# Pooled attention followed by a mixture-of-depths layer, one core: operations on different banks of one PSUM tile are declared independent

## The chip, the cores and the metric

The kernel runs on one core of one Trainium2 chip. The metric is the time of one launch on the device in microseconds (us). A second figure, the span, runs from the first to the last profiled instruction of the same execution.

## What is computed

The reference takes q, k and v of shape 8 batches x 8 heads x 576 tokens x 64. Keys and values are averaged over groups of 8 tokens, so each query attends to 72 pooled rows. The result, with the heads put side by side, is a row of 512 numbers per token; in each batch the 128 tokens with the highest gate score go through a small MLP, and its output is added to them.

```python
k_p = k.reshape(B, H, Sp, pool, D).mean(axis=3)
v_p = v.reshape(B, H, Sp, pool, D).mean(axis=3)
scores = scale * np.matmul(q, k_p.transpose(0, 1, 3, 2))
attn = np.exp(scores - max); attn = attn / (attn.sum + 1e-09)
x = (attn @ v_p).transpose(0, 2, 1, 3).reshape(B, S, 512)
scores = np.einsum('bsd,d->bs', x, w_gate)
for b in range(B):
    top_idx = np.argpartition(-scores[b], capacity)[:capacity]
    xe = x[b, top_idx]
    ye = np.maximum(xe @ w1, 0.0) @ w2
    g = 1.0 / (1.0 + np.exp(-scores[b, top_idx]))
    out[b, top_idx] = x[b, top_idx] + g[:, None] * ye
```

(w1 is 512 x 1024 and w2 is 1024 x 512; all data are float32.)

## The kernel before, in words

Everything that runs in this case is in `direct_path`; `general_path` stands behind a branch that the data do not take. Each batch b passes two parts. The front (`front(b)`) pools k (L507 on TensorE for batch 0, L518 and L519 on VectorE or GpSimd otherwise), transposes k and q (L527, L549), makes the scores in two halves (L567, L576), exponentiates them on ScalarE (L581, L585), pools v (L599, or L609 to L619), multiplies (L644, L648), divides by the row sums (`zs` L662 to L666, the reciprocal L670, `norm` L679 on ScalarE or L681 on VectorE), stores the 512-wide rows, and ranks the tokens: `score` (L697, L698), `spread` on TensorE (L718), a copy of the spread scores into `sr` (L398 on ScalarE, L400 on VectorE), five counts (L730), a one-hot matrix (L737, L741), `pick` on TensorE (L747), then `token` (L751), `value` (L764), the row numbers (L755) and a gather of the chosen rows by GpSimd (L756). The dense part (`dense(b)`) transposes the gathered rows (`turn`, L777), copies them (`xg`, L398 or L400), multiplies with w1 (`up`, L786), applies the maximum with 0 (`relu`, L793 on ScalarE, L795 on VectorE), multiplies with w2 (`down`, L800), forms `y` on VectorE (L805) and scatters it by GpSimd (`put`, L809). A put waits for the put before it. At the very end eight small matmuls (`busy`, L828), a check of ranges (L835 to L848) and a branch follow.

The order of all operations, the PSUM bank of each job and the engine of those that may run on two are a written table (ORDER, HOMES, TURNS); `Plan.place` walks it and issues operation after operation, and each engine executes its own in that order. A job is a chain of operations on the same bank or banks: TensorE writes, then VectorE or ScalarE reads.

PSUM has eight banks, held in three tiles: `pG` is banks 0 to 3, `pA` banks 4 and 5, `pJ` banks 6 and 7. `single(j)` and `pair(j)` give the view of a job's bank. Which instruction must wait for which is not written in the kernel: the recording layer derives it from the tiles that each instruction reads and writes. In the kernel before, an instruction on one bank of `pG` waits for an earlier instruction of another engine on another bank of `pG` just as for one on its own bank; the same holds for `pA` and `pJ`.

Of the kernel before, what the change touches and what calls it, by code (L numbers as in the profile page):

```python
# [101 lines left out]
ON_PE = (0,)  # L102


class Plan:
# [125 lines left out]
    def place(self):  # L231
# [10 lines left out]
        for n in order:  # L242
            e = ops[n]["eng"]
            self.before = last.get(e)
            if ops[n]["alts"]:
                ops[n]["fn"](e)
            else:
                ops[n]["fn"]()
            last[e] = ops[n]["mark"]


def direct_path(ctx, tc, q, k, v, moe_w_gate, moe_w1, moe_w2, moe_capacity, out, flag):
# [117 lines left out]

    out_rows = out.rearrange("b s d -> (b s) d")
# [127 lines left out]
    def pool_k(b):  # L499
        x = KR.rearrange("p (r t) d -> p r t d", t=4)  # L500
        if b in ON_PE:
            for n, (a, z) in enumerate(((0, 5), (5, 9))):
                j_ = plan.job(ONES)

                def sums(a=a, z=z, j_=j_):
                    for t in range(4):
                        nc.tensor.matmul(single(j_)[:, 0 : D * (z - a)], ident, x[:, a:z, t], start=(t == 0), stop=(t == 3))  # L507
# [45 lines left out]
    def scores(b, h):  # L553
# [8 lines left out]
        def go():  # L562
            for j in range(2):
                for r in range(4):
                    rows = slice(32 * r, 32 * r + 32)
                    for s in range(2):
                        nc.tensor.matmul(pG[64 * s : 64 * s + 64, r, 0:n], KT[i][rows, j, s, 0:NK],  # L567
                                         tokens(j, s, rows, 0, hi - lo), start=(j == 0), stop=(j == 1))
        add("PE", 0.03 + n * 3.55e-3, go, [("KT", i), ("QT", i, h)], [], 100 * b + 10 * h, mode=3264, job=j_, name=f"s{b}{h}")

        def rest():
            for j in range(2):
                for s in range(2):
                    for u, (a, z) in enumerate(SUB[h]):
                        x = 64 * s + 32 * u
                        nc.tensor.matmul(pG[x : x + 32, 0, n : n + w], KL[i][:, j, s].rearrange("p n m -> p (n m)"),  # L576
                                         tokens(j, s, slice(0, 128), a - lo, z - lo), start=(j == 0), stop=(j == 1))
        add("PE", 0.05 + w * 3.35e-3, rest, [("KL", i), ("QT", i, h)], [], 100 * b + 10 * h, mode=12832, job=j_, name=f"sl{b}{h}")

        def ex():  # L580
            nc.scalar.activation(EM[h][i], pG[:, :, 0:n], AF.Exp, scale=exp_scale)  # L581
        add("ACT", 0.03 + 4 * n * 0.985e-3, ex, [], [("EM", h, i)], 100 * b + 5, job=j_, name=f"x{b}{h}")

        def exl():
            nc.scalar.activation(EL[h][i], pG[:, 0, n : n + w], AF.Exp, scale=exp_scale)  # L585
# [47 lines left out]
    def attend(b, c):  # L633
# [5 lines left out]
        def go():  # L639
            acc = pair(j_)  # L640
            for m in range(NP):
                for s in range(2):
                    for z in range(halves):
                        nc.tensor.matmul(acc[64 * z : 64 * z + 64, s, E * m : E * m + E], EM[h][i][64 * s : 64 * s + 64, m, m0 + 64 * z : m0 + 64 * z + 64],  # L644
                                         VS[i][64 * s : 64 * s + 64, m, :], start=(m == 0), stop=False, skip_group_check=True)
            for s in range(2):
                for z in range(halves):
                    nc.tensor.matmul(acc[64 * z : 64 * z + 64, s, 0 : NP * E], EL[h][i][64 * s : 64 * s + 64, l0 + 64 * z : l0 + 64 * z + 64],  # L648
                                     VL[i][64 * s : 64 * s + 64, u].rearrange("p m e -> p (m e)"),
                                     start=False, stop=True, skip_group_check=True)  # L650
# [7 lines left out]
        def zs(e):  # L658
            o = view()
            z, g = (x.rearrange("p (s m) -> p s m", s=2) for x in (ZA[rows, b, c], SS[i][rows, c]))  # L660
            if e == "ACT":
                nc.scalar.activation(z, o[:, :, :, D], AF.Identity, bias=eps[rows])  # L662
                nc.scalar.copy(out=g, in_=o[:, :, :, D + 1])
            else:
                nc.vector.tensor_scalar(z, o[:, :, :, D], 1e-9 * POOLW, None, op0=OP.add)
                nc.vector.tensor_copy(g, o[:, :, :, D + 1])  # L666
# [6 lines left out]
        def norm(e):  # L673
            rz, o = RZ[i][rows, c], view()
            to = XS[i][c][rows].rearrange("p (m s d) -> p s m d", s=2, d=D)
            if e == "ACT":
                for s in range(2):
                    for m in range(NP):
                        nc.scalar.activation(to[:, s, m], o[:, s, m, 0:D], AF.Copy, scale=rz[:, NP * s + m : NP * s + m + 1])  # L679
            else:  # L680
                nc.vector.tensor_tensor(out=to, in0=o[:, :, :, 0:D],  # L681
                                        in1=rz.rearrange("p (s m one) -> p s m one", s=2, one=1).to_broadcast([n, 2, NP, D]),
                                        op=OP.mult)
# [8 lines left out]
    def rank(b):  # L692
# [18 lines left out]
        for half, (a, z) in enumerate(((0, 3), (3, NC))):  # L711
# [33 lines left out]
        def pick():  # L745
            for c in range(NC):
                nc.tensor.matmul(single(j_)[0:cap, 0:5], OH[:, c, :], AUX[i][:, c, :], start=(c == 0), stop=(c == NC - 1))  # L747
        add("PE", 0.25, pick, ["OH", ("AUX", i)], [], p - 70, job=j_, name=f"pk{b}")

        def token():  # L750
            nc.vector.tensor_reduce(out=TK[x], in_=single(j_)[0:cap, 0:2], axis=AX.X, op=OP.add)  # L751
# [485 lines left out]
```

## Time and profile before

| | us |
|---|---|
| median of the 2 runs shown | 292.2 |
| lowest and highest of them | 290.26, 294.14 |
| the profiled execution, its own time | 293.1 |
| its span | 291.3 |
| TensorE busy in the span | 235.7 |
| VectorE busy in the span | 151.6 |

The profiled execution is 0.9 us over the median. Its time is the span and 1.8 us outside it. In the rows further down, PE is TensorE, PEld its loading of weights, DVE VectorE, ACT ScalarE, POOL GpSimd and SP the engine that only issues transfers. A row of the timeline gives a start, a length and in brackets the idle time of the engine just ahead of the instruction, with the instruction whose end released it. PEclk is the TensorE clock that was granted, 1.00 being 2.4 GHz and 0.50 being 1.2 GHz.

### The profile page before, as it was taken

What the parts mean: (1) busy time and instruction counts of PE and PEld (TensorE: products, weight loads), DVE (VectorE), ACT (ScalarE), POOL (GpSimd) and SP (SyncE); (2) the same over time, 40 slices, a digit from 0 to 9 for tenths busy, and PEclk for the clock granted to TensorE, in tenths of its full rate; (3) what the DMA queues carried; (4) which work ended last, traced back from release to release, by engine and by line L of the source; (5) the groups of instructions that cost most, each with busy time, mean ns of one, the idle gap of its engine ahead of it and who ended that gap; (6) DMA issues with size and microseconds to landing.
All of it is one profiled execution on the core that took longest, in us unless ns stands there. A gap on an engine that the chain in (4) does not pass through costs nothing.

```text
span 291.3 us, 7374 instructions
## 1 busy us (share of the span) xinstructions
PE 235.7 (81%) x3074; PEld 163.1 (56%) x3074; DVE 151.6 (52%) x346; ACT 89.2 (31%) x302; POOL 96.2 (33%) x154
## 2 busy tenths in 40 slices
PE   4789559975499798999969889989939998897680
PEld 4576328644278347847745458546828767384240
DVE  5039997938386485787681767484540180001310
ACT  1013461873226545402464333643120001101000
POOL 4004587418730551160634541330531100201310
PEclk9599956989599999999999999999986999999697
DMA  5996798999994556599576200140245000100201
GB/s 185 294 318 195 255 334 301 347 285 284 369 345 166 207 177 214 158 316 309 174 238 230 66 2 2 47 121 16 97 119 170 7 32 0 36 2 0 102 6 47
DMA packets 18413, 47.88 MB, mean 164 GB/s; under 512 B 2964, under 2 KB 2964, under 8 KB 17476
## 3 DMA queue, kind: packets, MB, share of 16 engines
q1 hardware_dynamic: 13776, 37.75, 40.1%
q0 software_dynamic: 2896, 6.76, 7.1%
q10 hardware_dynamic: 1700, 2.82, 3.2%
q8 instruction: 26, 0.43, 0.6%
q14 instruction: 15, 0.12, 0.1%
HBM read 35.78 MB, written 11.53 MB: 162 GB/s over the span
## 4 chain that ended last, share of the span: by engine, by line
PE 43%; issue 17%; DMA 10%; DVE 9%; POOL 4%; ACT 2%; ACTq 0%; SPq 0%; POOLq 0%; DVEq 0%
PE pJ L786 9%; PE pJ L800 8%; DMA xr<-out_dram,ix 6%; PE pG L786 4%; PE pG L800 4%; PE pG L567 4%; DMA out_dram<-y,ix 3%; PE pG L644 2%; PE pA L644 2%; PE pG L576 2%; PE pG L648 2%; DMA vr<-in_v_dram 1%; PE pA L648 1%; DVE y L805 1%; DVE ss L697 1%
## 5 line engine op out<-in xcount | busy, mean ns | idle before, releaser
L786 PE MATMUL pJ<-xg,w 128*128 128x128 f32 x352 | 44.2, 279 | 5.2 <-DVE ht L795 2.1
L786 PEld LDWEIGHTS pJ<-xg,w 128*128 128x128 f32 x352 | 41.2, 192 | 11.6 <-issue 4.0
L730 DVE SCALAR_TENSOR_TENSOR cmp<-sr,sc,lat 128x576 bf16<-128x576 f32 (+1 forms) x40 | 37.6, 940 | 4.9 <-ACT sr L398 4.2
L800 PE MATMUL pJ<-w,ht 128*128 128x512 f32 x64 | 29.9, 602 | 3.5 <-issue 2.1
L567 PE MATMUL pG<-qt,kt 32*64 32x256 f32 (+1 forms) x512 | 22.5, 451 | 3.6 <-issue 2.0
L549 DVE STREAM_TRANSPOSE qt<-qr 128x1280 f32<-128x1280 f32 (+1 forms) x16 | 21.7, 1361 | 2.1 <-DMA qr<-in_q_dram 2.1
L755 POOL TENSOR_SCALAR ix<-tk 128x1 int32<-128x1 f32 x8 | 2.3, 285 | 60.5 <-DVE tk L751 25.8
L800 PE MATMUL pG<-w,ht 128*128 128x512 f32 x32 | 17.5, 699 | 5.7 <-DVE y L805 4.8
L581 ACT ACTIVATE em<-pG 128x1280 f32<-128x1280 f32 (+1 forms) x16 | 18.1, 1129 | 8.4 <-PE pG L576 8.4
L800 PEld LDWEIGHTS pJ<-w,ht 128*128 128x128 f32 x64 | 11.3, 190 | 14.7 <-issue 12.6
L609 POOL TENSOR_TENSOR vr<-vr 128x512 f32<-128x512 f32 (+1 forms) x11 | 16.6, 1525 | 1.3 <-DMA vr<-in_v_dram 1.3
L809 POOL DMA_INDIRECT out_dram<-y,ix x8 | 8.4, 1048 | 26.2 <-DVE y L805 23.0
L567 PEld LDWEIGHTS pG<-qt,kt 32*64 32x64 f32 x512 | 10.5, 141 | 11.6 <-issue 7.4
L800 PE MATMUL pA<-w,ht 128*128 128x512 f32 x32 | 16.7, 625 | 0.0
L644 PEld LDWEIGHTS pG<-vs,em 64*64 64x64 f32 x528 | 12.5, 144 | 7.1 <-issue 2.3
L786 PE MATMUL pG<-xg,w 128*128 128x128 f32 x128 | 15.5, 277 | 1.0 <-ACT ht L793 0.7
L786 PEld LDWEIGHTS pG<-xg,w 128*128 128x128 f32 x128 | 14.9, 192 | 2.2 <-issue 1.0
L644 PE MATMUL pG<-vs,em 64*64 64x66 f32 x528 | 14.0, 234 | 2.2 <-DVE ss L666 0.7
L800 PEld LDWEIGHTS pG<-w,ht 128*128 128x128 f32 x32 | 6.9, 226 | 14.7 <-issue 8.0
L679 ACT ACTIVATE xs<-pA,rz 128x64 f32<-128x64 f32 (+1 forms) x64 | 14.0, 342 | 2.2 <-DVE rz L670 1.3
L679 ACT ACTIVATE xs<-pG,rz 128x64 f32<-128x64 f32 x48 | 10.5, 329 | 12.9 <-DVE xs L681 6.8
L644 PEld LDWEIGHTS pA<-vs,em 64*64 64x64 f32 x480 | 11.2, 139 | 3.8 <-issue 2.6
(173 smaller groups left out, 397.6 us busy)
## 6 DMA issues: line engine op xcount, KB each, us to landing
vr<-in_v_dram SPq DMA_DIRECT2D x32, 256.0 KB
kr<-in_k_dram SPq DMA_DIRECT2D x7, 1152.0 KB
qr<-in_q_dram SPq DMA_DIRECT2D x8, 640.0 KB
qr<-in_q_dram SPq DMA_DIRECT2D x8, 512.0 KB
w<-in_moe_w_dram SPq DMA_DIRECT2D x4, 1024.0 KB
out_dram<-xs SPq DMA_DIRECT2D x15, 256.0 KB
out_dram<-xs ACTq DMA_DIRECT2D x9, 256.0 KB
vr<-in_v_dram SPq DMA_DIRECT2D x32, 64.0 KB
```

What stands on the lines that cost most here:

```text
L549: nc.vector.transpose(out=QT[b % 2][h].rearrange("p j t c -> p t j c"), in_=QR[b % 2][h].rearrange("p t (j e) -> p t j e", j=2))
L567: nc.tensor.matmul(pG[64 * s : 64 * s + 64, r, 0:n], KT[i][rows, j, s, 0:NK], tokens(j, s, rows, 0, hi - lo), start=(j == 0), stop=(j == 1))
L576: nc.tensor.matmul(pG[x : x + 32, 0, n : n + w], KL[i][:, j, s].rearrange("p n m -> p (n m)"), tokens(j, s, slice(0, 128), a - lo, z - lo) ...
L581: nc.scalar.activation(EM[h][i], pG[:, :, 0:n], AF.Exp, scale=exp_scale)
L609: engine(e).tensor_tensor(out=x[:, a:z, 0:4], in0=x[:, a:z, 0:4], in1=x[:, a:z, 4:8], op=OP.add)
L644: nc.tensor.matmul(acc[64 * z : 64 * z + 64, s, E * m : E * m + E], EM[h][i][64 * s : 64 * s + 64, m, m0 + 64 * z : m0 + 64 * z + 64], VS[ ...
L648: nc.tensor.matmul(acc[64 * z : 64 * z + 64, s, 0 : NP * E], EL[h][i][64 * s : 64 * s + 64, l0 + 64 * z : l0 + 64 * z + 64], VL[i][64 * s ...
L679: nc.scalar.activation(to[:, s, m], o[:, s, m, 0:D], AF.Copy, scale=rz[:, NP * s + m : NP * s + m + 1])
L730: nc.vector.scalar_tensor_tensor(cmp[0:n], SR[0:n], SC[i][0:n, c : c + 1], LAT[0:n, LAST - OFF[c] : LAST - OFF[c] + S], op0=OP.subtract, o ...
L786: nc.tensor.matmul(single(ju)[:, cap * f : cap * f + cap], w1[g][:, d, 128 * f : 128 * f + 128], XG[i][:, d, :], start=(d == 0), stop=(d = ...
L800: nc.tensor.matmul(single(jd)[0:cap, :], HT[i][f // 4][:, f % 4, :], w2[f // 4][:, f % 4, :], start=(f == 0), stop=(f == FB - 1))
L809: j = nc.gpsimd.indirect_dma_start(out=out_rows, out_offset=bass.IndirectOffsetOnAxis(ap=IX[x][:, :1], axis=0), in_=Y[i], in_offset=None)
```

## The change

`Plan.place` now keeps, beside the operation that is being issued, its engine, its job and the operations that it needs by the plan. A new function `note` is called with each instruction that touches PSUM. It looks back over the last 500 noted instructions of the same PSUM tile, and where the earlier one ran on another engine, is not among the operations needed, and has no bank in common, it declares that there is no dependency between the two. The 30 or so places where PSUM is written or read are wrapped in `note(...)`; nothing else changes.

```diff
+AGO = 500
...
-            self.before = last.get(e)
+            self.before, self.now = last.get(e), (n, e, ops[n]["job"], ops[n]["deps"])
...
+    beside = {}
+
+    def note(ins):
+        n, e, j, needs = plan.now
+        if j is None:
+            return
+        mine = plan.bank[j]
+        seen_ = beside.setdefault(max(mine[0], 2) // 2, [])
+        for m, x, theirs, d in seen_[-AGO:]:
+            if e != d and m not in needs and not set(mine) & set(theirs):
+                tc.declare_no_dep(ins.ins, x.ins, reason="another bank")
+        seen_.append((n, ins, mine, e))
...
     def copy(e, to, of):
         if e == "ACT":
-            nc.scalar.copy(out=to, in_=of)
+            note(nc.scalar.copy(out=to, in_=of))
         else:
-            nc.vector.tensor_copy(to, of)
+            note(nc.vector.tensor_copy(to, of))
...
-                nc.tensor.matmul(single(jd)[0:cap, :], HT[i][f // 4][:, f % 4, :], w2[f // 4][:, f % 4, :],
-                                 start=(f == 0), stop=(f == FB - 1))
+                note(nc.tensor.matmul(single(jd)[0:cap, :], HT[i][f // 4][:, f % 4, :], w2[f // 4][:, f % 4, :],
+                                 start=(f == 0), stop=(f == FB - 1)))
...
-            nc.vector.scalar_tensor_tensor(Y[i], single(jd)[0:cap, :], GV[x], XR[x], op0=OP.mult, op1=OP.add)
+            note(nc.vector.scalar_tensor_tensor(Y[i], single(jd)[0:cap, :], GV[x], XR[x], op0=OP.mult, op1=OP.add))
```

No instruction is added, removed or moved on any engine; only the waits differ. In the built program 57 of TensorE's 1,635 instructions, 32 of VectorE's 305, 29 of ScalarE's 317, 2 of GpSimd's 153 and 3 of SP's 114 wait for something else than before. Part of these differences are waits that an earlier instruction of the engine took care of before, and that now stand at the instruction that truly needs them. The lines below the inserted code are 14 higher in the changed kernel (L800 becomes L814).

Three places show it. The rows name the engine whose progress is waited for, not the instruction. The first is TensorE from the last `up` of batch 7 to its `down`, the kernel's last large piece of work; `down` writes bank 3 of `pG`, and `y` of batch 6 reads bank 0 of it (`ht_144` and `ht_145` are the two halves of the relu's output). Before:

```order
L786 MATMUL pJ<-xg_141,w_148 128x128 x8
L800 MATMUL pA<-w_151,ht_145 128x512 x3
L800 MATMUL pG<-w_150,ht_144 128x512 [waits DVE_49]
L800 MATMUL pG<-w_150,ht_144 128x512 x3
L800 MATMUL pG<-w_151,ht_145 128x512 x4
```

and now:

```order
L800 MATMUL pJ<-xg_141,w_148 128x128 x8
L814 MATMUL pA<-w_151,ht_145 128x512 x3
L814 MATMUL pG<-w_150,ht_144 128x512 [waits Activation_49]
L814 MATMUL pG<-w_150,ht_144 128x512 x3
L814 MATMUL pG<-w_151,ht_145 128x512 [waits Activation_49]
L814 MATMUL pG<-w_151,ht_145 128x512 x3
```

Nothing moved. The wait for VectorE (for `y` of batch 6) is gone, and in its place stand the waits for the two relus of batch 7 on ScalarE.

The second is VectorE at the end: `value` and `token` of batch 7, then `y` of batches 4, 5, 6 and 7 with the reciprocals of their gates between them. Before:

```order
L764 TENSOR_REDUCE gv_135<-pG 128x1 [waits PE_49,Activation_49]
L751 TENSOR_REDUCE tk_127<-pG 128x1 [waits Activation_49]
L768 RECIPROCAL gv_132<-gv_132 128x1 [waits Pool_49]
L805 SCALAR_TENSOR_TENSOR y_146<-pA,gv_132,xr_136 128x512 [waits DMASW0_49,DMASW5_49,DVE_49,PE_49]
...
L805 SCALAR_TENSOR_TENSOR y_147<-pA,gv_133,xr_137 128x512 [waits DMASW2_49,DMASW1_49,DVE_49]
L805 SCALAR_TENSOR_TENSOR y_146<-pG,gv_134,xr_138 128x512 [waits DMASW6_49,DMASW0_49,Activation_49]
```

and now:

```order
L778 TENSOR_REDUCE gv_135<-pG 128x1 [waits PE_49]
L765 TENSOR_REDUCE tk_127<-pG 128x1
L782 RECIPROCAL gv_132<-gv_132 128x1 [waits Pool_49]
L819 SCALAR_TENSOR_TENSOR y_146<-pA,gv_132,xr_136 128x512 [waits DMASW5_49,DMASW0_49,DVE_49]
...
L819 SCALAR_TENSOR_TENSOR y_147<-pA,gv_133,xr_137 128x512 [waits DMASW1_49,DMASW2_49,DVE_49,PE_49]
L819 SCALAR_TENSOR_TENSOR y_146<-pG,gv_134,xr_138 128x512 [waits DMASW6_49,DMASW0_49]
```

Again the order is the same. `y` of batch 4, on bank 4, no longer waits for TensorE's last writes to bank 5, which are the `down` of batch 5; that wait now stands at `y` of batch 5, which reads them. `token` of batch 7 no longer waits for a relu on ScalarE.

The third is TensorE where batch 5 is turned and batch 7 is spread over `pG`, between the `up` of batch 4 and that of batch 5. Before:

```order
L786 MATMUL pG<-xg_140,w_149 128x128 x15
L777 MATMUL pG<-ident,xr_137 128x128 [waits DMASW1_49,Activation_49]
L777 MATMUL pG<-ident,xr_137 128x128 x3
L800 MATMUL pA<-w_150,ht_142 128x512 [waits DVE_49]
L718 MATMUL pG<-ident,sc_114 128x128 [waits DVE_49]
L718 MATMUL pG<-ident,sc_114 128x128 x2
L786 MATMUL pA<-xg_141,w_148 128x128 x8
```

and now:

```order
L800 MATMUL pG<-xg_140,w_149 128x128 x15
L791 MATMUL pG<-ident,xr_137 128x128 [waits DMASW1_49,Activation_49]
L791 MATMUL pG<-ident,xr_137 128x128 x3
L814 MATMUL pA<-w_150,ht_142 128x512 [waits DVE_49]
L732 MATMUL pG<-ident,sc_114 128x128 [waits DVE_49]
L732 MATMUL pG<-ident,sc_114 128x128 x2
L800 MATMUL pA<-xg_141,w_148 128x128 [waits DVE_49,Activation_49]
```

The spread's wait has kept its engine but not its instruction: before, it is for a relu (L795), the ninth VectorE instruction after the score sum of batch 7; now it is for that sum itself (L698, now L712). The turn's wait for ScalarE is unchanged, but the ScalarE instruction in front of it, `norm` of batch 7 (L679), no longer waits for the last matmul of the `up` of batch 4 on another bank of `pG`.

## Rows read from the trace of the kernel before

**Rows 1.** The page: span, busy time by engine, TensorE's clock and DMA by slices.

```profile
span 291.3 us, 7374 instructions
...
PE 235.7 (81%) x3074; PEld 163.1 (56%) x3074; DVE 151.6 (52%) x346; ACT 89.2 (31%) x302; POOL 96.2 (33%) x154
...
PEclk9599956989599999999999999999986999999697
DMA  5996798999994556599576200140245000100201
```

**Rows 2.** Windows: stretch, length, busy time by engine, PEclk, DMA share, GB/s.

```profile
20.00:44.00 24.00, 16.94 (x352) 10.91 (x352) 23.14 (x38) 10.81 (x41) 13.73 (x13) 0.83 0.83 270
44.00:78.00 34.00, 24.85 (x512) 18.29 (x511) 21.74 (x40) 16.18 (x65) 20.63 (x33) 0.80 0.99 313
95.00:200.00 105.00, 93.78 (x1434) 60.60 (x1434) 67.73 (x161) 44.17 (x153) 39.65 (x54) 1.00 0.48 157
200.00:267.31 67.31, 59.21 (x410) 44.26 (x401) 18.05 (x60) 8.40 (x23) 10.76 (x23) 0.95 0.17 52
217.55:223.42 5.87, 5.87 (x22) 4.84 (x23) 0.00 (x0) 0.68 (x2) 1.30 (x2) 0.50 0.58 178
267.31:272.11 4.80, 0.00 (x1) 0.01 (x1) 2.59 (x7) 0.60 (x1) 2.30 (x3) 0.91 0.14 55
272.11:278.03 5.92, 5.92 (x7) 2.52 (x8) 0.70 (x3) 0.00 (x0) 1.04 (x2) 0.50 0.23 89
278.03:282.17 4.14, 4.14 (x12) 1.88 (x11) 0.00 (x0) 0.00 (x0) 0.00 (x0) 1.00 0.00 0
```

**Rows 3.** Timeline of PE: seven instructions that stood behind a wait.

```profile
76.52 0.87 PE L777 MATMUL pA<-ident,xr 128*128 128x128 f32 x3 [6.60 <-DMA xr<-out_dram,ix]
97.69 0.67 PE L800 MATMUL pJ<-w,ht 128*128 128x512 f32 x1 [2.10 <-issue]
149.61 0.60 PE L786 MATMUL pJ<-xg,w 128*128 128x128 f32 x3 [2.07 <-DVE ht L795]
162.12 0.66 PE L777 MATMUL pJ<-ident,xr 128*128 128x128 f32 x4 [0.63 <-DMA xr<-out_dram,ix]
212.61 0.66 PE L777 MATMUL pG<-ident,xr 128*128 128x128 f32 x4 [1.83 <-ACT xs L679]
217.55 0.69 PE L718 MATMUL pG<-ident,sc 128*128 128x128 f32 x2 [3.42 <-DVE ht L795]
272.11 10.06 PE L800 MATMUL pG<-w,ht 128*128 128x512 f32 x16 [4.80 <-DVE y L805]
```

**Rows 4.** Timeline of DVE: four waits, then two of the counts.

```profile
19.11 0.42 DVE L400 COPY ks<-pG 128x256 f32<-128x256 f32 x1 [12.40 <-PE pG L599]
66.04 0.16 DVE L751 TENSOR_REDUCE tk<-pJ 128x1 f32<-128x2 f32 x1 [4.93 <-ACT sr L398]
267.34 0.75 DVE L805 SCALAR_TENSOR_TENSOR y<-pA,gv,xr 128x512 f32<-128x512 f32 x1 [18.95 <-PE pA L800]
282.21 0.75 DVE L805 SCALAR_TENSOR_TENSOR y<-pG,gv,xr 128x512 f32<-128x512 f32 x1 [9.36 <-PE pG L800]
...
113.43 0.81 DVE L730 SCALAR_TENSOR_TENSOR cmp<-sr,sc,lat 128x576 bf16<-128x576 f32 x1
145.25 2.36 DVE L730 SCALAR_TENSOR_TENSOR cmp<-sr,sc,lat 128x576 bf16<-128x576 f32 x1
```

**Rows 5.** Timeline of POOL: an addition of v, then the last puts.

```profile
145.45 1.54 POOL L614 TENSOR_TENSOR vr<-vr 128x640 f32<-128x640 f32 x1
...
271.12 1.06 POOL L809 DMA_INDIRECT out_dram<-y,ix  x1 [1.39 <-DVE y L805]
274.69 0.96 POOL L809 DMA_INDIRECT out_dram<-y,ix  x1 [2.51 <-issue]
283.24 0.96 POOL L809 DMA_INDIRECT out_dram<-y,ix  x1 [7.58 <-DVE y L805]
```

**Rows 6.** DMA issues: count and median time to landing of the gathers.

```profile
xr<-out_dram,ix POOLq DMA_INDIRECT x8, 3.5
```

More of the change, by code (lines that the diff above doesn't have):

```diff
@@ L506, in sums @@
                     for t in range(4):
-                        nc.tensor.matmul(single(j_)[:, 0 : D * (z - a)], ident, x[:, a:z, t], start=(t == 0), stop=(t == 3))
+                        note(nc.tensor.matmul(single(j_)[:, 0 : D * (z - a)], ident, x[:, a:z, t], start=(t == 0), stop=(t == 3)))
                 add("PE", 0.05 + (z - a) * 0.43, sums, [("KR", n), "ident"], [], 100 * b - 60 + n, job=j_, name=f"kP{b}{n}")
@@ L566, in go @@
                     for s in range(2):
-                        nc.tensor.matmul(pG[64 * s : 64 * s + 64, r, 0:n], KT[i][rows, j, s, 0:NK],
-                                         tokens(j, s, rows, 0, hi - lo), start=(j == 0), stop=(j == 1))
+                        note(nc.tensor.matmul(pG[64 * s : 64 * s + 64, r, 0:n], KT[i][rows, j, s, 0:NK],
+                                         tokens(j, s, rows, 0, hi - lo), start=(j == 0), stop=(j == 1)))
         add("PE", 0.03 + n * 3.55e-3, go, [("KT", i), ("QT", i, h)], [], 100 * b + 10 * h, mode=3264, job=j_, name=f"s{b}{h}")
@@ L661, in zs @@
             if e == "ACT":
-                nc.scalar.activation(z, o[:, :, :, D], AF.Identity, bias=eps[rows])
-                nc.scalar.copy(out=g, in_=o[:, :, :, D + 1])
-            else:
-                nc.vector.tensor_scalar(z, o[:, :, :, D], 1e-9 * POOLW, None, op0=OP.add)
-                nc.vector.tensor_copy(g, o[:, :, :, D + 1])
+                note(nc.scalar.activation(z, o[:, :, :, D], AF.Identity, bias=eps[rows]))
+                note(nc.scalar.copy(out=g, in_=o[:, :, :, D + 1]))
+            else:
+                note(nc.vector.tensor_scalar(z, o[:, :, :, D], 1e-9 * POOLW, None, op0=OP.add))
+                note(nc.vector.tensor_copy(g, o[:, :, :, D + 1]))
         both((("DVE", 0.42), ("ACT", 0.45)), False, zs, ["eps"], [("Z", b, c), ("SS", i, c)], 100 * b - 35, job=j_, name=f"z{b}{c}")
@@ L827, in go @@
             for x in range(4):
-                nc.tensor.matmul(single(j_)[:, 128 * x : 128 * x + 128], ident, ident, start=True, stop=True)
+                note(nc.tensor.matmul(single(j_)[:, 128 * x : 128 * x + 128], ident, ident, start=True, stop=True))
         add("PE", 0.9, go, ["ident"], [], 1e4, job=j_, name=f"busy{i}")
@@ L842, in range_test @@
         j_ = plan.job(ONES)
-        add("PE", 0.2, lambda: nc.tensor.matmul(single(j_)[0:1, 0:2], ones, seen, start=True, stop=True),
+        add("PE", 0.2, lambda: note(nc.tensor.matmul(single(j_)[0:1, 0:2], ones, seen, start=True, stop=True)),
             ["seen0", "seen1", "ones"], [], 2050, job=j_, mode=12832, name="sum")
         def verdict():
-            nc.vector.scalar_tensor_tensor(match, single(j_)[0:1, 0:2], 1.0, want, op0=OP.mult, op1=OP.is_equal, accum_out=good)
+            note(nc.vector.scalar_tensor_tensor(match, single(j_)[0:1, 0:2], 1.0, want, op0=OP.mult, op1=OP.is_equal, accum_out=good))
             nc.vector.tensor_scalar(flag, good, 1.5, None, op0=OP.is_lt)
```

42 lines of the change are left out of this document (21 added, 21 removed).

## The prediction

> **What bounds the kernel now.** I read the page first. TensorE is busy 235.7 of 291.3 us, and no other engine is near that [rows 1]. So the time is TensorE's work, its pauses, and what lies ahead of and behind them. The slices show where its clock falls: at the start, at some places before 80 us, and twice near the end, the last time just ahead of the end. DMA is full up to about 80 us and light afterwards.
>
> The windows give the pauses by stretch [rows 2]. From 95 to 200 us TensorE is busy 93.78 of 105.00, so 11.2 are pauses, at full clock (1.00, that is 2.4 GHz). From 200 to 267.31 it is busy 59.21 of 67.31, so 8.1 are pauses. In 267.31 to 272.11 it does nothing for 4.80. Then comes a stretch at 0.50 (1.2 GHz): 7 passes of the last `down` take 5.92 us, where the other 9 of its 16 take 4.14 once the clock is back. At full clock the 7 would take 7 x 4.14 / 9 = 3.2; the records of half-clock work halve to 2.96, so 2.7 to 3.0 are lost there. A second stretch at 0.50, of 5.87 us from 217.55 on, loses half, 2.9.
>
> The timeline of TensorE says what ended the pauses [rows 3]. Next to each I put what the instruction truly needs by its bank. 149.61 is an `up` on `pJ` released by a relu. 212.61 is a turn behind a `norm` that itself stood behind an `up` on another bank of `pG`. 217.55 is a spread released by a relu which is not its input. 272.11 is the `down` of batch 7 released by `y` of batch 6, which reads another bank. Only 76.52 and 162.12 are released by what they need, gathered rows. From 95 to 200 us there are twelve pauses ended by an instruction on another bank, together 9.8 of the 11.2, and the two largest are 2.10 and 2.07.
>
> The timeline of VectorE has the same kind of wait [rows 4]: `y` of batch 4 stands at the head of the engine for 18.95 us, until 267.34, for `down` writes of batch 5 on the other bank of `pA`. The last `y` waits for the last `down` and GpSimd's last put for that `y` [rows 4, 5]. From that put at 283.24 to the end of the span are 291.3 - 283.24 = 8.06 us. That is the chain that sets the end.
>
> **The change part by part.** No instruction is added, removed or moved, so every term is a wait. The sum is made against the profiled execution, 293.1 (its span and 1.8), which is 0.9 over the median.
>
> *The end, from 267.31 us.* The 4.80 goes: both halves of the relu of batch 7 read banks that are written before 267.31, so the `down` that now waits for them can follow the one before it. With no pause ahead, I expect the stretch at half clock to go too, for 2.96. Together 7.76: the `down` would end at 282.17 - 7.76 = 274.4. Its `y` takes 0.75 and starts at about 274.45; the put follows 0.28 behind, as now (283.24 against 282.21 + 0.75), at 275.5. What is late next is the puts: each waits for the one before it, 271.12 to 274.69 = 3.57 apart [rows 5]. `y` of batch 4 is set free early, and its put with it. But `y` of batch 5 truly needs the `down` that ends at 267.31, so puts of batches 5, 6 and 7 stand at about 268.4, 271.95 and 275.5. Both ways give 275.5 in place of 283.24. I take 7.7. If the clock fell nevertheless, it is 4.8; no reason gives a loss, as the puts are the same ones.
>
> *200 to 267.31 us.* Ends: only the two large pauses go, 1.83 + 3.42 = 5.3; or all 8.1 and the lost clock, 8.1 + 2.9 = 11.0. I take the two pauses, the clock (which fell after them) and half of the other 2.85, that is 5.25 + 2.9 + 1.4 = 9.5. What covers it: VectorE is busy only 18.05 of 67.31 there and ScalarE 8.40 [rows 2], so a producer without its false wait is early at once. What is late next is the gather of the rows of a batch, which takes 3.5 us to land in the median [rows 6]. Its row numbers come from `token`, which loses false waits as well.
>
> *95 to 200 us.* Ends: the two large pauses, 4.2; or all twelve, 9.8. Here VectorE is busy 67.73 and GpSimd 39.65 of 105.00 [rows 2], so a wait removed is often followed by a true one close behind. Of the ten small pauses (9.8 - 4.2 = 5.6) I take a third: 4.2 + 1.9 = 6.1. The 0.63 ahead of the turn at 162.12 I leave.
>
> *Before 95 us.* Ends: nothing; or the whole pause of 6.60 at 76.52, ahead of the first turn. `token` of batch 0 waits 4.93 at 66.04 for a copy into `sr`, on another bank [rows 4], so the gather behind it can start earlier. But it shares the DMA engines, which are at 0.99 from 44 to 78 us, and an earlier issue need not land as much earlier. In the opening a copy of `ks` at 19.11 waits for matmuls on another bank; it is idle time of 12.40, but VectorE is full behind it (23.14 of 24.00 [rows 2]), and what it does later is bound by its own work and the loads. I take 2.0, nearer to nothing.
>
> Sum: 7.7 + 9.5 + 6.1 + 2.0 = 25.3. 293.1 - 25.3 = 267.8, and with the 0.9 between this execution and the median 266.9: **267 us**.
>
> **The rivals.**
>
> *The pauses in the middle refill.* When all engines move up, VectorE and GpSimd meet at other places. A count takes 0.81 us at 113.43 and 2.36 us at 145.25, where an addition of v on GpSimd lies beside it [rows 4, 5]: 1.55 more. Six such meetings more, one for each batch whose counts lie in the middle, are 9.3. Counted from the other side: the end's 7.7, the low end of 200 to 267.31 (5.3) and half of the two large pauses (2.1) are 15.1, so 293.1 - 0.9 - 15.1 = **277 us**. For it: VectorE's load up to 200 us. Against: after 200 us nothing is crowded.
>
> The Trainium skill, "SBUF — State Buffer", section "Who interferes with whom", says that a VectorE instruction with two inputs in SBUF contends with a GpSimd instruction that reads SBUF, and that the one that comes second is blocked until the first is done. The trace agrees in length: the addition ends at 146.99 and the count 0.62 behind that, at 147.61. It does not agree in order, as the count is recorded as the first to start.
>
> *It goes deeper.* The twelve pauses, the whole 11.0 and half of the 6.60 arrive: 7.7 + 11.0 + 9.8 + 3.3 = 31.8, so 293.1 - 0.9 - 31.8 = **260 us**. Against it: each stretch would have to reach its upper end.
>
> *The waits only move.* What is removed at one instruction is met at the next true one, close behind, and the end is held by something I have not seen: **290 us**. Against it: the rows at 272.11 and 267.34 name their releasers, and those are on other banks.
>
> *Slower: TensorE outruns the gathers and loses its clock at the turns.* The pauses are then not gone but gathered into eight longer ones, one ahead of each batch's turn. The clock has fallen after 1.83 + 3.42 within a few us and after 4.80, and not after 2.10 or 2.07 [rows 2, 3]. Each fall costs 2.9. If all eight turns met one, 8 x 2.9 = 23.2 against the end's 7.7 gives 292.2 + 23.2 - 7.7 = **308 us**. It decides, past 2%, from five such falls on (5 x 2.9 - 7.7 = 6.8). For it: a gather takes 3.5 to land, more than 2.10. Against: other work of TensorE lies ahead of most turns, and `token`, ahead of the gather, gets earlier too.
>
> **How the numbers follow.** The forecast, 261 to 274 us, has 0.62. The refilled case, 274 to 286, has 0.20; the deeper one, below 261, 0.09; no change, 286 to 298, 0.06; slower 0.03. A measurement of this kernel tells about 2%, 5.8 us, from no change. So faster is 0.62 + 0.20 + 0.09 = 0.91, same 0.06, slower 0.03. The range 259 to 281 takes all of the forecast, over half of the refilled case and some of the deeper one, 0.8.
>
> **What would show it.** In the changed kernel's profile: (1) `y` of batch 4 stands tens of us before `y` of batch 5, and the last `down` follows the `down` ahead of it without a pause, at full clock throughout; if its 16 passes take 10 us again, the clock term is wrong. (2) The last three puts are 3.6 apart, and 8.06 lie behind the last. (3) No stretch at half clock at the spread of batch 7, and under 2 us of pauses where 8.1 were. (4) Pauses from the first turn to batch 5's of about 5 where 11.2 were, ended by gathers or counts; if these reach 9, the refilled case is right, and counts of 2 us and more should be more frequent. (5) The first turn's pause is between 4 and 6.6. I would be wrong altogether if the new pauses stood ahead of the turns with the clock falling behind them.

## The result and the profile after

| | us |
|---|---|
| median of the 2 runs of the changed kernel | 262.8 |
| lowest and highest of them | 261.54, 264.04 |
| ratio to before, 95% interval | 0.899 (0.868 to 0.931) |
| the profiled execution, its own time | 264.0 |
| its span | 262.3 |

A later measurement, four more runs of the changed kernel beside seven of the kernel before, gave 0.9075 (0.900 to 0.915). So the change takes 27 to 29 us off. (The ratios here and below leave disturbed runs out, so they can differ a little from the ratio of two medians.) It was forecast at 267, with 259 to 281 as its range.

The page of the changed kernel; TensorE's row, then the clock and DMA by slices, to set against [rows 1]:

```profile
span 262.3 us, 7373 instructions
...
PE 225.8 (86%) x3074; PEld 158.2 (60%) x3074; DVE 150.5 (57%) x346; ACT 88.1 (34%) x302; POOL 99.9 (38%) x154
...
PEclk9999979999799599999999979999999999999995
DMA  5999999999997768499968510013116520110120
```

TensorE's busy time fell by 10, though it does the same work: half clock is the reason that the rows show. Not all of the 10 belongs to the change: in second profiles of both kernels (before_again and after_again below) it is 231.9 and 227.7. In the clock's row the low places towards the end are gone, except for the last slice, in which TensorE has nothing left to do; the lowest that remains is the 14th slice, from 85 to 92 us. DMA is full from the second slice on. It had gaps in the profile of [rows 1], but the second profile of the kernel before has none there either (6999899999 in the first ten slices), so they are not the change's doing.

Windows of the changed kernel, cut where TensorE is at the same instruction as at the borders of [rows 2]. Columns as there.

```profile
67.30:89.76 22.46, 19.11 (x306) 13.93 (x303) 13.37 (x27) 8.43 (x25) 10.64 (x14) 0.82 0.87 311
89.76:189.20 99.44, 93.09 (x1416) 61.23 (x1418) 72.13 (x160) 42.24 (x146) 40.43 (x54) 0.97 0.52 167
189.20:245.25 56.05, 55.10 (x435) 42.37 (x427) 18.25 (x63) 8.10 (x23) 12.37 (x25) 1.00 0.22 67
245.25:252.25 7.00, 7.00 (x19) 3.17 (x18) 2.14 (x5) 0.60 (x1) 2.03 (x2) 1.00 0.20 75
```

The first stretch, 78.00 to 95.00 in the kernel before, was 17.00 and is 22.46: the changed kernel enters it 10.7 ahead and leaves it 5.2 ahead. The second was 105.00 and is 99.44, the third 67.31 and is 56.05, and the last `down` with the pause ahead of it was 4.80 + 5.92 + 4.14 = 14.86 and is 7.00. The pauses went from 11.2 to 6.35, from 8.1 to 0.95 and from 4.80 to none, and the last two stretches run at 1.00 throughout.

The timeline of TensorE, the pauses that are left and the last `down`, to set against [rows 3]:

```profile
66.80 0.63 PE L791 MATMUL pA<-ident,xr 128*128 128x128 f32 x4 [2.62 <-DVE qt L563]
82.96 0.43 PE L732 MATMUL pJ<-ident,sc 128*128 128x128 f32 x2 [1.47 <-ACT ht L807]
86.35 1.16 PE L658 MATMUL pG<-vs,em 64*64 64x66 f32 x32 [1.88 <-ACT em L595]
...
90.22 4.47 PE L814 MATMUL pJ<-w,ht 128*128 128x512 f32 x8
...
152.05 0.65 PE L791 MATMUL pJ<-ident,xr 128*128 128x128 f32 x4 [2.69 <-DMA xr<-out_dram,ix]
...
152.87 3.21 PE L814 MATMUL pJ<-w,ht 128*128 128x512 f32 x4
...
201.01 0.49 PE L732 MATMUL pG<-ident,sc 128*128 128x128 f32 x3
...
245.22 7.03 PE L814 MATMUL pG<-w,ht 128*128 128x512 f32 x16
```

The spread at 201.01 and the `down` at 245.22 have no bracket: they follow the instruction ahead of them at once, where 3.42 and 4.80 stood. The largest pause behind 90 us is at a turn, for gathered rows. The pauses at 82.96 and 86.35 do not stand in the profile of the kernel before; they wait for ScalarE, and the passes behind them (4.47 for eight) are slower than there (3.67). The first is for a relu of batch 0, for which TensorE waits with the old opening too: 0.69 in both profiles of the kernel before, 1.92 in filler and 1.97 in late_only below.

VectorE's last `y` and GpSimd's last puts in the changed kernel, to set against [rows 4, 5]:

```profile
225.97 0.75 DVE L819 SCALAR_TENSOR_TENSOR y<-pA,gv,xr 128x512 f32<-128x512 f32 x1
245.42 0.75 DVE L819 SCALAR_TENSOR_TENSOR y<-pA,gv,xr 128x512 f32<-128x512 f32 x1 [10.77 <-PE pA L814]
...
252.28 0.75 DVE L819 SCALAR_TENSOR_TENSOR y<-pG,gv,xr 128x512 f32<-128x512 f32 x1 [4.69 <-PE pG L814]
```

The puts, by the timeline of GpSimd:

```profile
246.45 1.06 POOL L823 DMA_INDIRECT out_dram<-y,ix  x1 [12.12 <-DVE y L819]
250.02 0.96 POOL L823 DMA_INDIRECT out_dram<-y,ix  x1 [2.51 <-issue]
253.49 0.96 POOL L823 DMA_INDIRECT out_dram<-y,ix  x1 [2.50 <-DVE y L819]
```

`y` of batch 4 now stands 19.45 ahead of `y` of batch 5, and the three puts are 3.57 and 3.47 apart.

### The profile page after: what moved, and what is told of

It reads as the page before. It is cut to its first block, busy times and chain, and to the rows that moved or that the text cites. A ratio compares the mean times of both kernels' runs of the same rounds, so it can differ in the third digit from the quotient of the medians.

```text
span 262.3 us, 7373 instructions
## 1 busy us (share of the span) xinstructions
PE 225.8 (86%) x3074; PEld 158.2 (60%) x3074; DVE 150.5 (57%) x346; ACT 88.1 (34%) x302; POOL 99.9 (38%) x154
## 4 chain that ended last, share of the span: by engine, by line
DMA 38%; PE 37%; issue 7%; DVE 5%; POOL 5%; SPq 2%; ACT 2%; ACTq 0%; POOLq 0%; DVEq 0%
DMA qr<-in_q_dram 10%; PE pJ L800 9%; DMA vr<-in_v_dram 9%; DMA out_dram<-y,ix 6%; DMA w<-in_moe_w_dram 5%; PE pG L814 5%; PE pJ L814 4%; PE pG L800 4%; DMA out_dram<-xs 4%; DMA xr<-out_dram,ix 4%; PE pG L581 3%; PE pA L814 3%; SPq L400 2%; PE pA L658 2%; PE pG L590 2%
## 5 line engine op out<-in xcount | busy, mean ns | idle before, releaser
L800 PEld LDWEIGHTS pJ<-xg,w 128*128 128x128 f32 x352 | 41.6, 194 | 5.9 <-issue 5.1
L800 PE MATMUL pJ<-xg,w 128*128 128x128 f32 x352 | 43.6, 280 | 0.0
L744 DVE SCALAR_TENSOR_TENSOR cmp<-sr,sc,lat 128x576 bf16<-128x576 f32 (+1 forms) x40 | 36.6, 916 | 1.3 <-ACT sr L412 0.7
L814 PE MATMUL pJ<-w,ht 128*128 128x512 f32 x64 | 31.9, 636 | 0.0
L684 DVE RECIPROCAL rz<-za 128x8 f32<-128x8 f32 (+1 forms) x40 | 7.4, 190 | 20.9 <-ACT za L676 17.9
L814 PEld LDWEIGHTS pJ<-w,ht 128*128 128x128 f32 x64 | 11.9, 201 | 11.5 <-issue 11.1
L581 PEld LDWEIGHTS pG<-qt,kt 32*64 32x64 f32 x512 | 10.5, 138 | 11.6 <-issue 7.7
L658 PE MATMUL pA<-vs,em 64*64 64x66 f32 x480 | 12.9, 224 | 3.8 <-issue 3.1
L814 PE MATMUL pA<-w,ht 128*128 128x512 f32 x32 | 15.8, 596 | 0.0
L800 PEld LDWEIGHTS pG<-xg,w 128*128 128x128 f32 x128 | 14.8, 192 | 1.0 <-issue 1.0
L800 PE MATMUL pG<-xg,w 128*128 128x128 f32 x128 | 15.2, 276 | 0.0
L814 PE MATMUL pG<-w,ht 128*128 128x512 f32 x32 | 14.4, 592 | 0.0
```

The source lines that it names most:

```text
L581: note(nc.tensor.matmul(pG[64 * s : 64 * s + 64, r, 0:n], KT[i][rows, j, s, 0:NK], tokens(j, s, rows, 0, hi - lo), start=(j == 0), stop=(j ...
L658: note(nc.tensor.matmul(acc[64 * z : 64 * z + 64, s, E * m : E * m + E], EM[h][i][64 * s : 64 * s + 64, m, m0 + 64 * z : m0 + 64 * z + 64] ...
L684: nc.vector.reciprocal(RZ[i][rows, c], ZA[rows, b, c])
L744: nc.vector.scalar_tensor_tensor(cmp[0:n], SR[0:n], SC[i][0:n, c : c + 1], LAT[0:n, LAST - OFF[c] : LAST - OFF[c] + S], op0=OP.subtract, o ...
L800: note(nc.tensor.matmul(single(ju)[:, cap * f : cap * f + cap], w1[g][:, d, 128 * f : 128 * f + 128], XG[i][:, d, :], start=(d == 0), stop ...
L814: note(nc.tensor.matmul(single(jd)[0:cap, :], HT[i][f // 4][:, f % 4, :], w2[f // 4][:, f % 4, :], start=(f == 0), stop=(f == FB - 1)))
```

## The experiments

The theory after the result: each stretch gives up its own false waits, and the stretches add up. The rivals: a lead won early is taken back later by transfers; the waits of one side (TensorE) carry the gain; half clock has a cause of its own. Results are given as the median, with the ratio to the kernel before, measured beside it, and the ratio's 95% interval; gains in microseconds are worked out from the ratios. Since stretches are compared below, this is the measure that all profiles share: when the first `down` of batch 0 starts, and how long it is from there to the last put.

| kernel | first `down` | last put | between |
|---|---|---|---|
| before | 97.69 | 283.24 | 185.55 |
| before_again | 91.58 | 277.79 | 186.21 |
| open_only | 93.15 | 278.77 | 185.62 |
| mid_only | 93.59 | 271.32 | 177.73 |
| late_only | 92.08 | 259.18 | 167.10 |
| tail_only | 92.57 | 271.84 | 179.27 |
| pe_only | 91.38 | 267.48 | 176.10 |
| readers_only | 97.77 | 264.60 | 166.83 |
| after | 90.22 | 253.49 | 163.27 |
| after_again | 91.20 | 254.17 | 162.97 |
| stores_on_sp | 86.91 | 255.13 | 168.22 |
| key_copy | 96.77 | 282.10 | 185.33 |
| filler | 93.65 | 278.52 | 184.87 |
| filler_short | 95.56 | 280.26 | 184.70 |

**One stretch at a time: open_only, mid_only, late_only.** The changed kernel, in which `note` declares nothing unless the operation being issued lies in a part of the written order (`plan.at` is its place there; 307 is the first `down`, 657 the first `up` of batch 4; 656, just ahead of it, touches no PSUM):

```diff
-        for m, x, theirs, d in seen_[-AGO:]:
+        for m, x, theirs, d in seen_[-AGO:] if plan.at < 307 else ():
```

with `307 <= plan.at < 656` and `plan.at >= 656` for the other two.

> Only operations issued ahead of the first down of batch 0 (about 95 us in the kernel before) are declared independent of other banks. Theory (gains of the stretches add up): at that point the changed kernel is 5.2 us ahead, having been 10.3 ahead at 78 us; later stretches stall as in the kernel before and can't take more than their own pauses, so 292.2 - 5.2 = 287. Rival 1 (my forecast's term for this stretch): 2.0, so 290. Rival 2 (what is won early is lost again at the gathers and loads behind): 292.

> Only operations issued between the first down of batch 0 and the first up of batch 4 (about 95 to 200 us) are freed. Theory (adding up): the lead of the changed kernel grows from 5.2 to 10.8 us there, 5.6, so 286.6. Rival (the lead grows there only because the front came early): under 3, so 289 to 292.

> Only operations issued from the first up of batch 4 on (about 200 us) are freed. Theory (adding up): 11.0 us up to the last down and 7.1 behind it, 18.1 in all, so 274. Rival (only the named pauses go there: 1.83 and 3.42 and the end's 7.7): 13, so 279.

Measured: 287.6 (0.980, 0.972 to 0.987), 281.2 (0.964, 0.958 to 0.970) and 272.0 (0.936, 0.929 to 0.944), against 291.2. In microseconds 5.9, 10.5 and 18.5, together 34.9, which is more than the 27 to 29 of the whole. Each part gives its share alone, so none needs the others. They overlap, so it is not true that they simply add up. The table tells where: from the first `down` on, mid_only is 7.8 shorter and late_only 18.5, 26.3 in all, and the changed kernel 22.3. And open_only's span behind the first `down` is that of the kernel before (185.62 and 185.55), so what the opening wins is at least kept there.

**key_copy: the copies of the first pooled keys alone.** The same edit with this condition:

```diff
+        for m, x, theirs, d in seen_[-AGO:] if plan.name[:3] == "kC0" else ():
```

> Only the copies of the pooled keys of batch 0 are freed, so that VectorE's copy at 19.11 us no longer waits for matmuls on another bank. Theory (VectorE is full from there to 44 us, so all that it does moves up with that copy): the scores of batch 0 start about 2 us earlier, and VectorE's work of the opening 3 us earlier; the end 2 to 3.3 us earlier, 289 to 290. Rival (the opening's lead comes from other waits, as the spreads and copies into sr): less than 1, 291.5 or more.

Measured: 288.5 against 291.2 (0.988, 0.981 to 0.994): 3.6 us, 1.6 to 5.6. By this the rival's "less than 1" is out. But the executions took 286.8, 287.3, 289.6 and 292.1, beside 290.5 to 293.4 of the kernel before, and the ratio rests on the first three. The profile is of the one at 292.1, and it does not show the theory's way. VectorE in it, at the freed copy (19.11 before) and at a transposition of q behind it:

```profile
14.07 0.42 DVE L415 COPY ks<-pG 128x256 f32<-128x256 f32 x1 [7.78 <-PE pG L522]
...
33.89 1.50 DVE L564 STREAM_TRANSPOSE qt<-qr 128x1280 f32<-128x1280 f32 x1
```

That transposition in the kernel before, and in the changed kernel:

```profile
34.42 1.50 DVE L549 STREAM_TRANSPOSE qt<-qr 128x1280 f32<-128x1280 f32 x1
```

```profile
31.54 1.50 DVE L563 STREAM_TRANSPOSE qt<-qr 128x1280 f32<-128x1280 f32 x1
```

The copy is 5.0 earlier, the transposition 0.5, and the first `down`, at 96.77, lies between those of the two profiles of the kernel before. So the times speak for a gain of a few microseconds; how it gets from the copy to the end is not shown.

**before_again and after_again: how steady is the opening?** No edit.

> The kernel before, unchanged, for a second profile of it. Theory (the first 95 us differ from execution to execution, since DMA brings the inputs there): the first down of batch 0 starts 2 to 6 us earlier than the 97.69 of the profile shown, while the time from there to the last down's end stays 184.5 within 0.5. Rival (the stretch is steady, and leads of 4 to 6 us at that point belong to the kernels that showed them): it starts within 1 us of 97.69.

> The changed kernel, unchanged, beside these. Theory: 262.8 within 2; the first down of batch 0 starts within 4 us of the 90.22 of its first profile, since the opening differs from execution to execution, and from there to the last put it is the same within 1 us (163.3). Rival (the opening is steady in this kernel): 90.22 within 0.5.

Measured: 288.1 for the single run of the kernel before, 263.8 for the changed one (median of four). The timeline of TensorE at the first `down`, in before_again:

```profile
91.58 5.28 PE L800 MATMUL pJ<-w,ht 128*128 128x512 f32 x8 [2.10 <-issue]
```

It starts at 91.58, where the profile shown had 97.69 [rows 3]: 6.1 us between two executions of one kernel. What follows is steadier, 185.55 and 186.21; to the end of the last `down` the two differ by 0.7, where 0.5 was expected. In the changed kernel the two profiles give 90.22 and 91.20, and 163.27 and 162.97 behind them, as expected. So a comparison of two profiles tells the gain behind the first `down` to some 2 us (that `down` alone takes from 3.67 to 5.33 in the profiles with all waits ahead of it), and ahead of it hardly at all: the seven profiles with the old opening (these two, mid_only, late_only, tail_only and the two fillers) start the `down` at 93.8 in the mean, from 91.6 to 97.7, and the three with the freed one (open_only and the two of the changed kernel) at 91.5, from 90.2 to 93.2.

**tail_only: the end alone.** The condition is `plan.name in ("y4", "y5", "y6", "y7") or plan.name[:2] == "d7"`.

> Only y of batches 4 to 7 and the down of batch 7 are freed. Theory (my forecast's term for the end: 4.80 of pause, 2.96 of half clock, put chain at 3.5 apart): 7.7 us less, 283.5 against 291.2. Rival (the clock doesn't come back with the pause): 4.8 less, 286.4. Rival (the puts hold the end): under 4 less, 287.5 or more.

Measured: 284.9 against 291.1 (0.982, 0.974 to 0.990), 5.3 us with 3.1 to 7.5 as its interval. By its trace, TensorE's last passes of batch 5 and the `down` of batch 7:

```profile
260.96 2.74 PE L815 MATMUL pA<-w,ht 128*128 128x512 f32 x6
263.54 7.03 PE L815 MATMUL pG<-w,ht 128*128 128x512 f32 x16
```

and its last puts on GpSimd:

```profile
264.78 1.07 POOL L824 DMA_INDIRECT out_dram<-y,ix  x1 [12.12 <-DVE y L820]
268.36 0.96 POOL L824 DMA_INDIRECT out_dram<-y,ix  x1 [2.51 <-issue]
271.84 0.96 POOL L824 DMA_INDIRECT out_dram<-y,ix  x1 [2.52 <-DVE y L820]
```

From the start of the last six passes of batch 5's `down` to the last put are 271.84 - 260.96 = 10.88; in the kernel before those passes start at 264.56, and the put at 283.24 is 18.68 behind. That is 7.8 us, for which 7.7 was forecast. From the first `down` on the table gives 6.3, as that `down` itself takes 5.31 here and 3.67 there. The interval of the times just fails to reach 7.7; the opening's scatter is a likely reason, not a shown one.

**filler and filler_short: is it the pause that halves the clock?** The kernel before, all waits in place, with work put into the last pause (32 in filler, 18 in filler_short):

```diff
             def down(f=f):
+                for x in range(18 if b == 7 and f == 0 else 0):
+                    nc.tensor.matmul(pJ[:, 0, 128 * (x % 4) : 128 * (x % 4) + 128], ident, ident, start=True, stop=True)
```

> The kernel before with all its waits; 32 matmuls of the identity (about 4.2 us by the 1.05 us of the eight at the end) are added on TensorE in the 4.80 us ahead of the down of batch 7. Theory (half clock comes from the pause and costs 2.96 there): the last down takes 7.0 to 7.2 us in place of 10.06, starts at the same place, and the end comes 3 us earlier, 288.2 against 291.2. Rival (half clock has another cause): 291.2, with the last down at 10.06.

> As the filler before, with 18 matmuls in place of 32. The 32 took 7.31 us, 0.23 each, and put the last down off by about 2.3; 18 take 4.1 and fit into the 4.80. Theory: the last down starts 4.8 us behind the down of batch 5 as in the kernel before and takes 7.03, so the end comes 2.8 to 3.0 earlier than there by its own trace, from the end of the down of batch 5; by the time 288.2 against 291.1. Rival (what the filler won was no clock): 291.1.

Measured: 289.9 (0.996, 0.989 to 1.003) and 289.4 (0.994, 0.986 to 1.002), neither clear of no change. The first was mis-sized: eight records of such matmuls are four of them, so the 32 took 7.31 us and put the `down` off, though it then took 7.03. The 18 of the second fit into the pause. Its time cannot tell 3 us from none, and its trace decides. TensorE's timeline in filler_short, with the 18 (36 records) in the second row:

```profile
264.52 2.74 PE L802 MATMUL pA<-w,ht 128*128 128x512 f32 x6
267.10 4.18 PE L801 MATMUL pJ<-ident 128*128 128x128 f32 x36
272.06 7.13 PE L802 MATMUL pG<-w,ht 128*128 128x512 f32 x16 [0.79 <-DVE y L807]
```

and the last put there:

```profile
280.26 0.96 POOL L811 DMA_INDIRECT out_dram<-y,ix  x1 [4.65 <-DVE y L807]
```

The `down` starts as late as before (272.06, 272.11 then) and takes 7.13 in place of 10.06; the last put is at 280.26 in place of 283.24, with the passes ahead at the same place (264.52, 264.56). The clock term is 2.9 by this trace, and it comes from the pause.

**pe_only and readers_only: whose waits carry the gain?** The condition is `e == "PE"`, and `e != "PE"` for the other.

> Only TensorE's instructions are freed; VectorE and ScalarE wait as in the kernel before. Theory (the pauses of TensorE are mostly its own false waits): at the end the last down follows at once, but y of batch 4 stands until its old place, so four puts 3.5 apart follow it and the end gains 4.2 of 7.7; of the 16 to 17 of the stretches from 95 us on some 13, and about 2 ahead of them: 272. Rival (the readers' false waits hold the same pauses up, so one side alone does little): over 280.

> Only the instructions of VectorE, ScalarE, GpSimd and SP are freed; TensorE waits as in the kernel before. Theory: at the end y of batch 6 comes about 1.5 us behind the down of batch 5, so the last down pauses 1.5 in place of 4.80 and stays at full clock, as after the 2.10 at 97.69; 6 of 7.7. In the stretches from 95 us on some 4, in the opening 2: 279. Rival (each side alone does little): over 283.

Measured: 275.2 (0.947, 0.940 to 0.954) and 274.2 (0.943, 0.937 to 0.949), against 290.0. At the end both did about what was expected: from the start of the last six passes of batch 5's `down` to the last put, pe_only gains 5.1 (4.2 expected) and readers_only 6.2 (6). pe_only's `down` follows at once, and its four puts then hold the end; readers_only's `down` waits 1.59 and stays at full clock. The puts of pe_only:

```profile
257.70 1.08 POOL L824 DMA_INDIRECT out_dram<-y,ix  x1 [14.01 <-DVE y L820]
260.43 1.06 POOL L824 DMA_INDIRECT out_dram<-y,ix  x1 [1.39 <-DVE y L820]
264.01 0.96 POOL L824 DMA_INDIRECT out_dram<-y,ix  x1 [2.51 <-issue]
267.48 0.96 POOL L824 DMA_INDIRECT out_dram<-y,ix  x1 [2.50 <-issue]
```

The last `down` of readers_only:

```profile
256.43 7.10 PE L815 MATMUL pG<-w,ht 128*128 128x512 f32 x16 [1.59 <-DVE y L820]
```

From 95 us on the theory had the shares the wrong way round. By the table pe_only is 9.5 shorter behind the first `down`, and readers_only 18.7, with 22.3 for both. Two places show how; they are 3.6 of the 9.2 between the two kernels. The first is the turn that stood 1.83 at 212.61 [rows 3], in pe_only and then in readers_only, where it has no bracket:

```profile
205.03 0.66 PE L792 MATMUL pG<-ident,xr 128*128 128x128 f32 x4 [1.84 <-ACT xs L694]
```

```profile
206.24 0.60 PE L792 MATMUL pG<-ident,xr 128*128 128x128 f32 x4
```

TensorE's own wait there is a true one. It is the `norm` on ScalarE that waited falsely, and only the readers' side frees it. The second is in pe_only `token` of batch 7 on VectorE, which still waits for a relu on another bank, and behind its gather the turn of that batch:

```profile
237.40 0.16 DVE L766 TENSOR_REDUCE tk<-pG 128x1 f32<-128x2 f32 x1 [2.29 <-ACT ht L808]
```

```profile
241.95 0.66 PE L792 MATMUL pJ<-ident,xr 128*128 128x128 f32 x4 [1.79 <-DMA xr<-out_dram,ix]
```

In the changed kernel neither that `token` nor that turn pauses. The two shares together are 28.2, for 22.3, so some 6 can be won from either side.

**stores_on_sp: the pauses at 82.96 and 86.35.** In the changed kernel two stores of batch 1 that ScalarE issues go to SP:

```diff
         self.bank = bank
         ops, last = self.ops, {}
+        for o in ops:
+            if o["name"] in ("o14", "o12"):
+                o["eng"] = "SP"
```

> The changed kernel with two stores of batch 1 (o14 and o12) issued by SP in place of ScalarE. Theory (in the changed kernel ScalarE stands 8.09 us at the issue of the second, until the first has landed, with a relu of batch 0 behind it, for which TensorE pauses twice, 1.47 and 1.88, and then runs at half clock): the relu comes about 4 us earlier, the two pauses and the half clock go, 3 to 5 us less, 258 to 260 against 262.8. Rival (the loads set this stretch, DMA being full until about 80 us): within 1 us of 262.8.

The timeline of ScalarE in the changed kernel (ACTq is its queue issuing a transfer):

```profile
71.16 0.57 ACTq L400 DMA_DIRECT2D out_dram<-xs  x1
...
73.31 0.18 ACT L677 COPY ss<-pA 128x8 f32<-128x8 f32 x1
81.59 0.62 ACTq L400 DMA_DIRECT2D out_dram<-xs  x1
82.31 0.60 ACT L807 ACTIVATE ht<-pJ 128x512 f32<-128x512 f32 x1 [8.82 <-DVE qt L563]
```

ScalarE's work ahead of the second store ends at 73.49. The releaser in the last bracket is inferred, and the relu reads nothing of it: it follows the issue of the store at once. The same relu in late_only names the store:

```profile
82.17 0.60 ACT L808 ACTIVATE ht<-pJ 128x512 f32<-128x512 f32 x1 [6.50 <-DMA out_dram<-xs]
```

Measured: 263.7 (0.907, 0.902 to 0.912 of the kernel before), as after_again (0.9075). By the trace the pauses are gone. The window from the first turn to the first `down` in the changed kernel:

```profile
66.80:90.22 23.42, 20.07 (x313) 14.58 (x314) 14.02 (x28) 8.89 (x27) 11.17 (x15) 0.82 0.89 310
```

The same in stores_on_sp:

```profile
69.03:86.91 17.88, 17.88 (x313) 13.60 (x314) 13.67 (x27) 8.04 (x23) 7.86 (x13) 0.90 0.92 323
```

And pauses that TensorE has behind it there, by its timeline:

```profile
99.29 0.63 PE L794 MATMUL pJ<-ident,xr 128*128 128x128 f32 x4 [1.61 <-DMA xr<-out_dram,ix]
...
126.11 1.12 PE L584 MATMUL pG<-qt,kt 32*64 32x256 f32 x32 [2.12 <-DVE qt L566]
```

The stretch is 5.5 shorter, as the theory had it, with no pause in it. But the time is the same: from the first `down` to the last put it takes 168.22 in place of 163.27. TensorE now pauses for gathered rows of batch 1 and for a transposition of q of batch 5. The windows place the loss: from the first `down` to an `up` that starts at 140.04 (137.79 in the changed kernel) it is 53.13 in place of 47.57, and behind that 0.6 less. Of the 5.6, 4.0 are pauses (those two and three of 0.54, 0.70 and 0.16, less 1.09 in the changed kernel), and TensorE is busy 1.5 longer. VectorE, at that transposition, in stores_on_sp and in the changed kernel:

```profile
124.72 1.25 DVE L566 STREAM_TRANSPOSE qt<-qr 128x1024 f32<-128x1024 f32 x1 [4.41 <-DMA qr<-in_q_dram]
```

```profile
124.08 1.25 DVE L563 STREAM_TRANSPOSE qt<-qr 128x1024 f32<-128x1024 f32 x1 [2.06 <-DMA qr<-in_q_dram]
```

TensorE was 3.3 ahead at the first `down`, and the load of q came no earlier. So the theory was right on the stretch and wrong on the time, and the rival right on the time: in this part transfers set the pace, and a lead ahead of them is taken back.

## Why the prediction was right

The terms, each from the windows of both kernels:

| stretch (of before) | forecast | measured |
|---|---|---|
| before 95 us | 2.0 | 95.00 - 89.76 = 5.2 |
| 95 to 200 | 6.1 | 105.00 - 99.44 = 5.6 |
| 200 to 267.31 | 9.5 | 67.31 - 56.05 = 11.3 |
| end | 7.7 | 14.86 - 7.00 = 7.9, less 0.9 behind it |
| sum | 25.3 | 29.0 |

*The end* came out step by step: no pause, full clock, 7.03 for the forecast's 7.1, puts about 3.5 apart, the last one 7.8 earlier from the same place. filler_short shows the clock term by itself (2.9 of it), tail_only the whole, and pe_only the chain of puts that it would have run into. Not foreseen: from the last put to the end of the span are 8.81 in place of 8.06. It is 8.41 in before_again and 9.03 in after_again; no run shows the cause.

*200 to 267.31* was taken half way into its small pauses. They went nearly all: 0.95 is left of 8.1, and the clock stayed. The reason given, that the producers have time there, was right, and late_only shows 18.5 for this stretch and the end without any lead from before.

*95 to 200* came within 0.5, but in part by luck. A third of the small pauses was taken, and about 5 us of pauses were to be left. In the changed kernel none of the twelve instructions pauses any more, which alone would be the deeper case's 9.8. But 6.35 stand at four others: 1.09 and 0.68 for a transposition of q and a `norm`, 2.69 and 1.89 ahead of turns, for gathered rows. So true waits took back over half of what the false ones gave, where the forecast had most of the small ones stay. The rival of refilled pauses had the refilling right, but wanted it from longer counts, with a gain of 2.1 here. The page's group of the 40 counts in the changed kernel has a mean of 916 ns:

```profile
L744 DVE SCALAR_TENSOR_TENSOR cmp<-sr,sc,lat 128x576 bf16<-128x576 f32 (+1 forms) x40 | 36.6, 916 | 1.3 <-ACT sr L412 0.7
```

It was 940 before, so the counts as a whole have not become longer. (By the timeline of the kernel before, the twelve pauses add up to 10.1 and not 9.8, and for the largest, the 2.10, it names no instruction but "issue".)

*Before 95* is the step that was mis-sized, 2.0 where the two profiles differ by 5.2. Two errors stand in it. The first is in the reading: that VectorE is full from 20 to 44 us was taken as a cover for its idle time ahead of that. It covers only a part. In the changed kernel the copy stands at 13.40, 5.7 earlier, and the transposition of 34.42 at 31.54, 2.9 earlier; in between VectorE now waits 1.20 for a load of q and 1.10 for ScalarE. The times give 3.6 us for this one wait (key_copy) and 5.9 for the stretch (open_only). The second is in the measure: the profile's opening was late by 6.1 against the next execution of the same kernel, and no single profile carries a term there. The sign for the first turn, a pause of 4 to 6.6, failed in one profile of the changed kernel (2.62) and held in the other (6.04). From 27 to 29 us in all, 22.3 from the first `down` to the last put and 0.8 lost behind that, the opening's share comes to 5.5 to 7.5; the means of the profiles differ by 2.3, and open_only's times give 5.9 with 3.7 to 8.1. A closer figure stays open.

The case that TensorE loses its clock at the turns came at one turn behind 95 us, the one at 152.05 with its 2.69. The `down` behind it took 3.21 for four passes, of which four take 1.88 at full clock (121.38), so the fall cost 1.3 in these passes, where the rival reckons 2.9 for each. A window in it:

```profile
154.00:156.00 2.00, 2.00 (x4) 0.80 (x3) 2.00 (x1) 1.63 (x9) 1.91 (x2) 0.50 0.14 57
```

The bounds of the range were needed on the deep side, where the result lies, between the forecast and the 260 of the deeper case.

## What to carry to other kernels

Dependencies that a framework derives from tiles are as coarse as the tiles: where one tile spans several banks, ask of each wait whether it names the data's own producer. Look upstream of a pause: its releaser may be a true producer that was itself late through a false wait, and freeing the waiting engine alone then gives less than freeing the others (9.5 against 18.7 here). An idle stretch of an engine ahead of a full one is not covered by it: what stands behind can move up until it meets a load (of 5.7 us 2.9 were left here). The gain of a stretch that transfers pace has to be measured in many executions, not in one profile.

## What the runs showed of the hardware

The opening, in which DMA is nearly full, differed by 6.1 us between two executions of the same kernel, with 185.55 and 186.21 behind it. The profile with the later `down` has gaps in its DMA row where the other has none; what made them was not looked for.

I had written that the clock does not fall after a pause of 2.10. In before_again the same eight passes after the same 2.10 take 5.28, where 3.67 stood in the first profile; the windows give the clock. Those passes in before_again:

```profile
91.58:96.86 5.28, 5.28 (x10) 2.35 (x11) 1.41 (x4) 2.06 (x11) 4.42 (x5) 0.69 0.89 306
```

and in the kernel before, as first profiled:

```profile
97.69:101.36 3.67, 3.67 (x10) 1.71 (x11) 1.41 (x4) 2.06 (x11) 3.67 (x4) 1.00 0.76 293
```

0.69 is a mean over a part at 1.2 GHz and a part at 2.4. So the clock may or may not be low behind a pause of this length, for 1.6 us, in one and the same kernel. It stayed up behind the 1.59 of readers_only (7.10 for the 16 passes) and fell behind the 2.69 of the changed kernel. That the pause is the cause is shown for the 4.80 alone, by filler_short.

A store that ScalarE issues can hold up the work behind it: ScalarE did nothing for 8.1 us, from the end of its work at 73.49 to the issue at 81.59, with a relu behind it for which TensorE was waiting. With the two stores on SP the pause of TensorE there is gone.
